# Loading q ahead of k and v for two batches, and scaling the last q of a batch behind the attends

## The chip, the cores and the metric

The kernel runs on one core of one Trainium2 chip. The metric is the device time of one execution in microseconds (us). The mean granted clock of TensorE is 1.000 in the profile of the kernel before. Engines: PE is TensorE, DVE is VectorE, ACT is ScalarE, POOL is GpSimd, SP is SyncE. Spans in a profile are about 1.7 us shorter than the times (986.4 and 988.09 us for the profiled run of the kernel before), because a span runs from the first to the last instruction.

## The reference

```python
# q, k, v: (8 batches, 8 heads, 576, 64)
phi(x) = concat(relu(x) * cos_w, relu(x) * sin_w)      # weights by position
kv  = einsum('bhsf,bhsd->bhfd', phi(k), v);  z = sum_s phi(k)
x   = (phi(q) @ kv) / (phi(q) . z + 1e-6)              # attention, then rows (4608, 512)
P   = sinkhorn(exp(x @ w_gate - max))                  # 8 rounds, 8 experts
out = sum_e P[:, e] * (relu(x @ w1[e]) @ w2[e])
```

The change touches the first stage only, in which the attention of eight batches is computed between the matmuls of the first expert.

## The kernel before

The first stage runs in blocks. Block `j` pushes 512 rows through the first expert's two matmuls in 16 slots: slots 0 to 7 make `h_ps` (four matmuls, then a ReLU on ACT into `hT`; there are two `h_ps` buffers), slots 8 to 15 make `y_ps`. After each slot's matmuls the work listed for that slot is issued, and it belongs to the attention of batch `j + 1` or prepares batch `j + 2`. In these traces an engine takes its work in the written order, so one instruction that waits holds up what stands behind it on its engine; the DVE wait of 2.23 us below, with `zsel` behind it, is an example.

The pieces that matter are these. A load brings two head pairs of q, k or v of one batch (288 KB) and is issued by POOL. `held_back` makes its issue wait for the last DVE instruction written so far. From batch 2 on, a scaled q is transposed by a DMA that SP issues, and there are three scaled-q buffers, so the fourth q waits until the first transpose is done.

Some words for what follows. A DMA has landed when all its data has arrived. The first and second sums of a batch are the key-value sums of its two halves (PE); from their last column DVE makes `zsel`, and "PE's wait for the key sums" is its wait for that `zsel` before the last 12 matmuls of the denominators. `hl` comes from the reciprocal of the denominators. In the profile, transposed q stand under `q_pT`, but two of the eight buffers lie in memory lent by `acc_lo` and `acc_hi` and carry these names, as do other tiles of this stage.

```python
ld      = tile_pool(name="ld", bufs=4)        # 2 batches of each of q, k, v
qp_pool = tile_pool(name="qp_pool", bufs=3)   # scaled q
...
def load(b, half, names="qkv", held_back=False):
    for name in names:
        x = ld.tile([P, 2, C, D], F16, name=f"{name}_ld")
        ...
        i = nc.gpsimd.dma_start(out=..., in_=view[:, 2 * half : 2 * half + 2])
        if held_back:
            after(ve.last, i)                 # wait for the last DVE work written
...
def prep_q(b, hk):
    q16 = loaded.pop(("q", b, hk))
    by_dma = b >= 2
    if by_dma:
        ve.tensor_scalar(out=q16, in0=q16, scalar1=0.0, scalar2=None, op0=ALU.max)
    q_p = qp_pool.tile([P, C, 2, D], F16, name="q_p")
    ve.tensor_tensor(out=q_p[:], in0=q16 (broadcast), in1=cs, op=ALU.mult)
    if by_dma:
        qTs[b, hk] = q_pTs[(b * HK + hk) % len(q_pTs)]
        nc.sync.dma_start(out=qTs[b, hk], in_=q_p[:]..., transpose=True)
...
# prep_k: ReLU of k on ACT.  prep_kv: scaled k and v copy, on DVE.
# sums: key-value sums on PE, `zsel` on DVE.  denominators(b): 24 matmuls over all of
# qTs[b], then a reciprocal on DVE.  attend(b, hk): PE, ACT and DVE write xT.
...
if j == 1:
    for hk in range(HK):
        ...
        at(j, 0, prep_kp, b, hk)
        at(j, (0, 0, 1, 3)[hk], prep_v, b, hk, ...)
        if hk == 1:
            for half in range(2):
                at(j, 0, load, b + 1, half, "qkv", True)
    at(j, 3, sums, b, 0)
    at(j, 5, sums, b, 1)
...
at(j, 6 if j == 1 else 3, denominators, b)
for hk in range(HK):
    at(j, (9, 10, 12, 13)[hk] if j == 1 else 6 + 2 * hk, attend, b, hk)
...
```

The rest of the program, most of its 987 us, is not touched by the change.

The softmax here doesn't subtract the row's maximum and nothing guards it: scores larger than these inputs give would overflow.

## Time and profile before

| | kernel before |
|---|---|
| time, median of 4 runs | 987.46 us (985.78 to 990.17) |
| span of the profile, clock | 986.4 us, 1.000 |
| block 1 (45.68 to 70.25) | 24.57 us |
| block 2 (70.25 to 93.08) | 22.83 us |
| blocks 3 to 5, each | 19.64 us |

A block here reaches from the first `h_ps` matmul of one block to that of the next, read off the timeline of PE. The chain that ended last says how much of the span belongs to whom. This is its line on the page of the kernel before:

```profile
PE 91%; issue 2%; ACT 2%; DVE 2%; DMA 2%; POOL 1%; ACTq 0%; DVEq 0%; POOLq 0%; SPq 0%
```

PE is the chain almost everywhere, so what can be won is PE's idle time. The next lines are the table by stretches of the kernel before, for blocks 1 and 2; the columns are the stretch, its length, the busy time and number of instructions of PE, of weight loads, of DVE, ACT and POOL, then PE's granted clock, the DMA share and GB/s.

```profile
45.68:70.25 24.57, 21.37 (x245) 10.62 (x243) 18.47 (x43) 14.92 (x32) 4.28 (x6) 1.00 0.92 151
70.25:93.08 22.83, 19.88 (x210) 9.99 (x205) 15.59 (x37) 12.59 (x31) 6.59 (x10) 1.00 0.92 133
```

PE stands idle for 3.2 us of block 1 and for 2.95 us of block 2. The timeline of PE in the kernel before shows where. The columns are start, length, engine, line, operation, tiles and shapes, count, and in brackets the idle time before it and what ended it.

```profile
55.16 0.56 PE L109 MATMUL small_ps<-q_pT,zsel 128*32 128x192 f16 x12 [0.72 <-DVE zsel L109]
58.69 0.42 PE L109 MATMUL small_ps<-hl,acc_hi 96*128 96x192 f16 x3 [0.28 <-DVE hl L109]
65.52 0.54 PE L109 MATMUL small_ps<-q_pT,kv_sb 128*64 128x384 f16 x4 [2.06 <-DVE xT L109]
...
79.84 1.02 PE L109 MATMUL h_ps<-xT,w1e 128*128 128x512 f16 x4 [2.19 <-ACT hT L109]
89.23 0.54 PE L109 MATMUL small_ps<-acc_hi,kv_sb 128*64 128x384 f16 x4 [0.76 <-DVE xT L109]
```

PE waited for DVE and ACT, and these in their turn waited for DMAs. These are the lines of the timelines of DVE, ACT and POOL in the kernel before that stand behind the waits:

```profile
53.87 0.31 DVE L109 TENSOR_SCALAR q_ld<-q_ld 128x576 f16<-128x576 f16 x1 [2.23 <-DMA q_ld<-in_q_dram]
64.24 0.76 DVE L109 TENSOR_TENSOR q_p<-q_ld,acc_hi 128x1152 f16<-128x1152 f16 x1 [2.97 <-DMA q_pT<-q_p]
78.62 0.68 ACT L109 ACTIVATE k_ld<-k_ld 128x576 f16<-128x576 f16 x1 [3.32 <-DMA k_ld<-in_k_dram]
49.65 0.72 POOL L201 DMA_DIRECT2D q_ld<-in_q_dram  x1 [16.73 <-DVE k_ld L109]
71.60 0.72 POOL L201 DMA_DIRECT2D q_ld<-in_q_dram  x1 [17.67 <-DVE zsel L109]
```

DVE waits for the first q of batch 3 (53.87), which stands before the `zsel` that PE needs. It waits again for a scaled-q buffer whose transpose has not ended (64.24), with an attend's `xT` behind it. ACT waits for k of batch 4 (78.62), with a ReLU behind it. The loads of batch 3 are issued from 49.65 on and those of batch 4 from 71.60 on. How long the first of them took from issue to landing, and a transpose issued before them, the views of these two tiles tell (POOL's q load at 49.65; SP's transpose at 47.4):

```profile
L201 POOL DMA_DIRECT2D q_ld<-in_q_dram x1: 716/716/716, 49.6 to 49.6; - x1
DMA to landing us min/median/max: 4.2/4.2/4.2
...
L360 SPq DMA_TRANSPOSE q_pT<-q_p x1: 1272/1272/1272, 47.4 to 47.4; - x1
DMA to landing us min/median/max: 4.9/4.9/4.9
```

### The profile page before, as it was taken

The numbers are of one execution on the slowest core, as the hardware profiler recorded it, in microseconds if no ns is written. First come the engines' busy times: TensorE is split into PE (matmuls) and PEld (weight loads), VectorE is DVE, ScalarE is ACT, GpSimd is POOL, SyncE is SP. The second block draws the span as 40 slices with busy tenths as digits, with TensorE's granted clock in tenths as the row PEclk, the third lists the DMA queues.
The fourth block names the chain that finished last, engine by engine and source line by source line (L and its number), as shares of the span: only waits on it lengthen the run. The fifth ranks groups of instructions, "written<-read, shape, count | busy, mean of one in ns | idle before, by whom it ended". The sixth has DMA issues, their size and how long they took to land.

```text
span 986.4 us, 20281 instructions
## 1 busy us (share of the span) xinstructions
PE 968.7 (98%) x7877; PEld 676.4 (69%) x7877; DVE 806.8 (82%) x1833; ACT 565.6 (57%) x1263; POOL 60.6 (6%) x82
## 2 busy tenths in 40 slices
PE   9988999989999999999999999999999999999997
PEld 6544444447777777777777777777777777777775
DVE  6765774789889888988789888988789888988887
ACT  5755665467776555555555555555555555555551
POOL 6122110010000000000000000000000000000001
PEclk9999999999999999999999999999999999999999
DMA  9989990642013410133113400133103401104435
GB/s 164 182 131 161 155 153 21 127 73 61 26 49 68 77 39 25 42 75 68 45 29 67 92 25 26 50 66 68 50 25 67 92 25 27 47 26 116 129 86 129
DMA packets 80336, 73.54 MB, mean 75 GB/s; under 512 B 33264, under 2 KB 72176, under 8 KB 80240
## 3 DMA queue, kind: packets, MB, share of 16 engines
q0 software_dynamic: 27232, 30.94, 20.1%
q1 hardware_dynamic: 52768, 41.06, 17.1%
q8 instruction: 61, 1.00, 0.4%
q14 instruction: 35, 0.29, 0.1%
q10 hardware_dynamic: 240, 0.26, 0.1%
HBM read 83.12 MB, written 12.98 MB: 97 GB/s over the span
## 4 chain that ended last, share of the span: by engine, by line
PE 91%; issue 2%; ACT 2%; DVE 2%; DMA 2%; POOL 1%; ACTq 0%; DVEq 0%; POOLq 0%; SPq 0%
PE rows_ps L109 34%; PE h_ps L109 27%; PE copied_ps L109 11%; PE p_ps L109 11%; PE y_ps L109 5%; PE small_ps L109 3%; DMA q_pT<-q_p 1%; DMA k_ld<-in_k_dram 1%; ACT hT L109 0%; DVE acc_hi L913 0%; POOL hs_last L928 0%; DVE P_tok L109 0%; DMA out_dram<-acc_lo 0%; DVE colp L109 0%; ACT u L109 0%
## 5 line engine op out<-in xcount | busy, mean ns | idle before, releaser
L913 DVE SCALAR_TENSOR_TENSOR acc_lo<-rows_ps,P_tok,acc_lo 128x512 f32<-128x512 f32 (+1 forms) x322 | 203.7, 642 | 74.7 <-PE rows_ps L109 74.6
L109 PEld LDWEIGHTS <-H 128*128 128x128 f16 x2080 | 203.0, 98 | 83.1 <-issue 1.2
L849 ACT CAST u<-h_ps 128x384 f16<-128x384 f32 x288 | 137.8, 479 | 131.1 <-PE h_ps L109 131.1
L109 PEld LDWEIGHTS <-w1e 128*128 128x128 f16 x1632 | 156.5, 98 | 68.9 <-issue 8.7
L843 DVE CUSTOM_DVE_ANT_0 H<-p_ps,u 128x384 f16<-128x384 f32 x329 | 181.6, 552 | 6.5 <-PE p_ps L109 6.4
L109 PEld LDWEIGHTS <-hs 128*128 128x128 f16 x1500 | 146.6, 98 | 56.2
L109 PE MATMUL h_ps<-S,w1e 128*128 128x384 f16 x672 | 164.1, 326 | 1.1 <-ACT u L109 0.9
L109 PE MATMUL p_ps<-xT,T 128*128 128x384 f16 x672 | 164.1, 326 | 0.1
L109 PE MATMUL h_ps<-xT,w1e 128*128 128x384 f16 (+1 forms) x616 | 150.0, 350 | 2.4 <-ACT hT L109 2.2
L109 PE MATMUL rows_ps<-V,H 128*128 128x256 f16 x1000 | 150.0, 273 | 0.7 <-DVE acc_hi L913 0.7
L109 PE MATMUL rows_ps<-w2e,hs 128*128 128x256 f16 x1000 | 150.0, 273 | 0.0
L881 ACT ACTIVATE H<-h_ps 128x384 f16<-128x384 f32 x144 | 70.8, 491 | 95.0 <-PE h_ps L109 95.0
L109 PEld LDWEIGHTS <-T 128*128 128x128 f16 x1008 | 98.1, 98 | 29.3 <-issue 2.8
L109 PE MATMUL rows_ps<-w2e,H 128*128 128x256 f16 (+1 forms) x568 | 91.2, 285 | 0.0
L862 ACT COPY copied_ps<-h_ps 128x384 f32<-128x384 f32 x144 | 67.5, 469 | 35.1 <-PE h_ps L109 35.1
L872 ACT ACTIVATE H<-copied_ps 128x384 f16<-128x384 f32 x144 | 70.9, 493 | 20.3 <-PE copied_ps L109 20.3
L109 PE MATMUL copied_ps<-xT,w1e 128*128 128x384 f16 x336 | 82.1, 326 | 0.0
L109 PE MATMUL h_ps<-S,T 128*128 128x384 f16 x336 | 81.8, 325 | 0.3 <-ACT copied_ps L109 0.3
L109 PE MATMUL copied_ps<-w2e,H 128*128 128x256 f16 x504 | 75.5, 272 | 0.0
L109 PE MATMUL rows_ps<-V,hs 128*128 128x256 f16 x500 | 74.9, 272 | 0.0
L913 DVE SCALAR_TENSOR_TENSOR acc_lo<-copied_ps,P_tok,acc_lo 128x256 f32<-128x256 f32 x126 | 60.3, 478 | 0.4
L913 DVE SCALAR_TENSOR_TENSOR acc_hi<-rows_ps,P_tok,acc_hi 128x512 f32<-128x512 f32 (+1 forms) x56 | 41.3, 738 | 20.5 <-PE rows_ps L109 19.7
(147 smaller groups left out, 955.2 us busy)
## 6 DMA issues: line engine op xcount, KB each, us to landing
S<-x_saved SPq DMA_DIRECT2D x108, 192.0 KB, 2.4
out_dram<-acc_lo SPq DMA_DIRECT2D x62, 128.0 KB, 2.4
w1e<-in_moe_w_dram POOLq DMA_DIRECT2D x7, 1024.0 KB, 9.3
w2e<-in_moe_w_dram POOLq DMA_DIRECT2D x7, 1024.0 KB, 9.6
q_ld<-in_q_dram POOLq DMA_DIRECT2D x16, 288.0 KB, 7.0
k_ld<-in_k_dram POOLq DMA_DIRECT2D x16, 288.0 KB, 8.0
v_ld<-in_v_dram POOLq DMA_DIRECT2D x16, 288.0 KB, 9.1
x_saved<-S SPq DMA_DIRECT2D x18, 192.0 KB, 1.9
```

The lines of the kernel that those rows point to most:

```text
L109: i = getattr(self.engine, name)(*args, **kwargs)
L843: latest = ve._custom_dve(TENSOR_ADD_SAT, out=out, in0=ps[:, 0:TU], in1=t[:], s0=FP32_MAX, s1=0.0)
L849: se.copy(out=t[:], in_=ps[:, 0:TU])
L862: se.copy(out=Y[:, 0:TU], in_=X[:, 0:TU])
L872: se.activation(out=h11, in_=Y[:, 0:TU], func=AF.Relu)
L881: se.activation(out=h12, in_=X[:, 0:TU], func=AF.Relu)
L913: ve.scalar_tensor_tensor(out=a, in0=rows, scalar=P_tok[:, g, self.e : self.e + 1], in1=a, op0=ALU.mult, op1=ALU.add,)
```

## The change

The intent is to have the loads of batches 3 and 4 (the fourth and the fifth) come earlier, with q first, but no earlier than the last scaled q of the batch in front, meant to keep them from overtaking that batch's transposes. The fourth scaled q of batch 3 goes behind all attends of block 1, so that its buffer wait cannot hold up an attend. In block 2 the k scalings are asked for one or two slots later (the first two by two), because k now comes third.

```diff
                 if j == 1:
+                    for name in "qkv":
+                        for half in range(2):
+                            at(j, 0, load, b + 1, half, name, True)
                     for hk in range(HK):
 ...
-                        if hk == 1:
-                            for half in range(2):
-                                at(j, 0, load, b + 1, half, "qkv", True)
 ...
-                    (8, prep_k, 1), (9, prep_q, 3), (10, prep_kv, 0), (10, prep_k, 2),
-                    (12, prep_kv, 1), (12, prep_k, 3), (13, prep_kv, 2), (14, prep_kv, 3),
+                    (8, prep_k, 1), (10, prep_kv, 0), (10, prep_k, 2), (12, prep_kv, 1),
+                    (12, prep_k, 3), (13, prep_q, 3), (14, prep_kv, 2), (14, prep_kv, 3),
                 ) if j == 1 else (
+                    (4, prep_q, 0), (5, prep_k, 0), (5, prep_q, 1), (6, prep_k, 1),
+                    (7, prep_q, 2), (8, prep_kv, 0), (8, prep_k, 2), (9, prep_q, 3),
+                    (10, prep_k, 3), (10, prep_kv, 1), (12, prep_kv, 2), (13, prep_kv, 3),
+                ) if j == 2 else (
                     (3, prep_k, 0), (4, prep_q, 0), (4, prep_k, 1), (5, prep_q, 1),
 ...
-            if j and b + 2 < B:
+            if j == 1:
+                for name in "qkv":
+                    for half in range(2):
+                        at(j, 13, load, b + 2, half, name, True)
+            elif j and b + 2 < B:
                 for half in range(2):
-                    at(j, (14 if j == 1 else 11) + half, load, b + 2, half, "qkv", True)
+                    at(j, 11 + half, load, b + 2, half, "qkv", True)
```

The change has three parts: A, the loads of batch 3; B, the fourth scaled q of batch 3 behind the attends (the third scaled k and v copy moves from slot 13 to 14 with it); C, the loads of batch 4 together with the new order in block 2.

## The prediction

> **What bounds the kernel now.** The chain of waits gives PE 91% of the span, at granted clock 1.000. The change touches only blocks 1 and 2 of the first stage. By the timeline of PE, blocks 3 to 6 last 19.64 us each with PE full; block 1 (45.7 to 70.25) lasts 24.6 us and block 2 (to 93.1) 22.9 us. Block 1 has one half of key-value sums more (0.7 us), so about 7.5 us over PE's own work is all there is to win.
>
> Where it goes (timelines of PE, DVE, ACT):
> - Block 1: DVE waits 2.23 us for q of batch 3 (53.85), delaying the key sums: PE 0.72 us, then 0.28 us for the reciprocal. DVE then waits 2.97 us for a scaled-q buffer whose transpose has not ended (64.2): PE 2.06 us, before an attend.
> - Block 2: ACT waits 3.32 us for k of batch 4 (78.6), holding up the ReLU: PE 2.19 us. A later wait for a transpose costs PE 0.76 us.
>
> **Loads and transposes.** Six loads, issued 0.71 us apart, take about 10.5 us of DMA traffic (51.5 to 62, packets by queue). A transpose alone lands in 3.2 to 3.4 us. One issued at 55.1 under the loads took 9.1: no packet of it moved before 59, then the two queues alternated about one for one. The Trainium skill ("DMA: Bandwidth & Descriptors", queues, rings and completion order) says each engine goes round-robin between its queues by packet; the counts from 59.5 to 61.5 agree, the silence before does not follow from it.
>
> **What the change does.** No operation is added or removed; order and holds differ.
> - Loads of batch 3 start at the last scaled q of batch 2 (DVE ends at 47.3) instead of 49.65. q comes first, both tiles by about 51.5 and 53: no DVE wait, about 1.0 us of PE.
> - The last scaled q of batch 3 goes behind all attends: its buffer is free by then, and a late transpose cannot block an attend: 2.06 us of PE.
> - Loads of batch 4 start at that scaled q, just before block 2 instead of 1.35 us into it. q before k eats part of this, but k is asked for two slots later: ACT's wait falls from 3.3 us to under 1.3, which the two h buffers absorb: about 2 us of PE.
> - Costs. The last transposes of batches 2 and 3 are now released together with the loads: landing goes from 4.9 and 3.2 us to 5 to 7. The denominators need them 6.8 us (block 1) and 5.3 us (block 2) after issue: 0 to 1.5 us, mainly in block 2. q before the last k scalings delays the second sums by 0.2 to 0.4. In block 2 the fourth q's buffer may come later: 0 to 0.5.
>
> Sum: block 1 minus 2.8, block 2 minus 2.0, all on the critical path: -4.8 us. 987.8 becomes **983.0 us**, range **980.0 to 987.0**. Faster by over 2%: 0.01; within 2%: 0.98; slower: 0.01.
>
> **Right if:** block 1 is 21 to 22.3 us and block 2 20 to 21.8; PE's waits of 2.06 and 2.19 us are gone; the first q load is issued near 47.3; blocks 3 to 6 stay 19.64.
>
> **Wrong if:** the denominators wait 2 us or more for a transpose that now shares the engines with the loads; k comes so late behind both q that ACT still holds PE; or spread (985.8 to 990.2) covers the gain.

## The result, and the profile after

The time fell from 987.46 to 983.85 us (medians of 4 runs each; 982.96 to 984.03 after). The ratio is 0.9959, 95% interval 0.9936 to 0.9983. Ratios are the mean time of one kernel's runs over that of the other's of the same rounds, so not quite the ratio of the medians. The interval lies clear of 1. The changed kernel was timed twice more as a control, with ratios 0.9958 and 0.9959.

| | before | after | control 1 | control 2 |
|---|---|---|---|---|
| span of the profile, us | 986.4 | 982.0 | 981.0 | 982.2 |
| start of block 1, us | 45.68 | 45.21 | 44.66 | 45.07 |
| block 1, us | 24.57 | 22.67 | 22.01 | 22.44 |
| block 2, us | 22.83 | 20.78 | 20.76 | 20.92 |

Blocks 1 and 2 together went from 47.40 to 43.45 us, so 3.95 of the 4.4 us by which the spans differ. Most of the rest is the start: block 1 begins 0.47 us earlier in this profile, where the change has done nothing yet. The chain line of the changed kernel and its table by stretches:

```profile
PE 93%; DVE 2%; ACT 2%; DMA 2%; issue 1%; POOL 0%; ACTq 0%; DVEq 0%; SPq 0%; POOLq 0%
...
45.21:67.88 22.67, 20.85 (x245) 10.13 (x244) 17.86 (x41) 14.69 (x32) 4.30 (x6) 1.00 0.97 151
67.88:88.66 20.78, 19.90 (x210) 9.84 (x205) 16.05 (x38) 12.61 (x31) 6.91 (x10) 1.00 1.07 163
```

The chain's share of PE does not tell the two kernels apart: it is 91% and 92% in the controls. PE's busy time in block 1 fell by 0.5 us too, all of it in the small groups of the attends (three of the four `kv_sb` groups show 0.54 us before, all four 0.44 us after); the record does not show how much of this is waiting that the profile counts as work. These are the waits that PE has left in blocks 1 and 2 of the changed kernel, by its timeline:

```profile
55.51 0.56 PE L109 MATMUL small_ps<-q_pT,zsel 128*32 128x192 f16 x12 [1.54 <-DVE zsel L109]
59.04 0.42 PE L109 MATMUL small_ps<-hl,acc_hi 96*128 96x192 f16 x3 [0.28 <-DVE hl L109]
...
69.81 0.46 PE L109 MATMUL small_ps<-acc_lo,k_p 64*128 64x65 f16 x18 [0.50 <-DVE acc_lo L109]
73.95 0.34 PE L109 MATMUL small_ps<-acc_hi,zsel 128*32 128x192 f16 x6 [0.38 <-DMA acc_hi<-q_p]
```

The two long waits (2.06 and 2.19 us) are gone. Two short new ones stand in block 2: the second sums wait for DVE, and the denominators for the last transpose. And one has doubled, from 0.72 to 1.54 us. The reason stands in the timelines of DVE, ACT and POOL:

```profile
54.22 0.31 DVE L109 TENSOR_SCALAR q_ld<-q_ld 128x576 f16<-128x576 f16 x1 [3.05 <-DMA q_ld<-in_q_dram]
77.64 0.68 ACT L109 ACTIVATE k_ld<-k_ld 128x576 f16<-128x576 f16 x1 [0.80 <-DMA k_ld<-in_k_dram]
47.12 1.43 POOL L201 DMA_DIRECT2D q_ld<-in_q_dram  x2 [14.27 <-DVE q_p L109]
68.00 1.43 POOL L201 DMA_DIRECT2D q_ld<-in_q_dram  x2 [16.58 <-DVE q_p L109]
```

The first q load was issued 2.5 us earlier (2.1 us, counted from the start of block 1), and DVE waited longer for it. Its landing time went from 4.2 to 7.1 us, and that of the transpose released with it from 4.9 to 5.9 us:

```profile
L201 POOL DMA_DIRECT2D q_ld<-in_q_dram x1: 713/713/713, 47.1 to 47.1; - x1
DMA to landing us min/median/max: 7.1/7.1/7.1
...
L360 SPq DMA_TRANSPOSE q_pT<-q_p x1: 1272/1272/1272, 46.9 to 46.9; - x1
DMA to landing us min/median/max: 5.9/5.9/5.9
```

So the size of the gain came out about as predicted, but one of its terms did not come: the earlier loads of q were to take a wait away and did not. The experiments ask what each part is worth, and why q came late.

### The profile page after: what moved, and what is told of

It reads as the page before. It is cut to its first block, busy times and chain, and to the rows that moved or that the text cites. A ratio compares the mean times of both kernels' runs of the same rounds, so it can differ in the third digit from the quotient of the medians.

```text
span 982.0 us, 20280 instructions
## 1 busy us (share of the span) xinstructions
PE 967.8 (99%) x7877; PEld 675.3 (69%) x7877; DVE 806.9 (82%) x1833; ACT 564.8 (58%) x1263; POOL 60.7 (6%) x82
## 3 DMA queue, kind: packets, MB, share of 16 engines
q1 hardware_dynamic: 52768, 41.06, 17.1%
## 4 chain that ended last, share of the span: by engine, by line
PE 93%; DVE 2%; ACT 2%; DMA 2%; issue 1%; POOL 0%; ACTq 0%; DVEq 0%; SPq 0%; POOLq 0%
PE rows_ps L109 34%; PE h_ps L109 27%; PE copied_ps L109 11%; PE p_ps L109 11%; PE y_ps L109 6%; PE small_ps L109 4%; DMA q_ld<-in_q_dram 1%; DMA acc_hi<-q_p 1%; ACT hT L109 0%; DVE xT L109 0%; DVE acc_hi L921 0%; POOL hs_last L936 0%; DVE P_tok L109 0%; DMA out_dram<-acc_lo 0%; ACT rb L109 0%
```

## The experiments

Twelve runs were made, two of them of the changed kernel as it is. All gave correct results but one. The runs of one call share their runs of the kernel before. Block lengths come from one profile of each kernel.

### First call: the control and the parts by themselves

The control is the changed kernel, unaltered.

> The changed kernel as it is, a control that shares its runs of the kernel before with the three below. Expected: block 1 (from the first to the second block's first h_ps matmul on PE) 22.7 us, block 2 20.8 us as in its first profile (the kernel before: 24.6 and 22.8), time ratio to before 0.996.

Measured: 982.95 us (982.75 to 983.49, 5 runs) against 987.19 us of the kernel before (986.23 to 988.49, 9 runs), ratio 0.9958 (0.9944 to 0.9971). DVE waited 2.39 us for q, PE 0.87 us for the key sums. The wait for q is thus longer than before in this profile too, but its size varies from run to run.

**Part B alone.** The kernel before, with this edit:

```diff
-                    (8, prep_k, 1), (9, prep_q, 3), (10, prep_kv, 0), (10, prep_k, 2),
-                    (12, prep_kv, 1), (12, prep_k, 3), (13, prep_kv, 2), (14, prep_kv, 3),
+                    (8, prep_k, 1), (10, prep_kv, 0), (10, prep_k, 2), (12, prep_kv, 1),
+                    (12, prep_k, 3), (13, prep_q, 3), (14, prep_kv, 2), (14, prep_kv, 3),
```

> The kernel before with one part of the change: in block 1 the fourth scaled q of batch 3 goes behind all attends (slot 13); loads and block 2 as before. Theory A (the three parts act separately): only PE's 2.06 us wait before an attend goes; the 0.72 us wait for the key sums stays; block 1 22.5 us; block 2 22.8 us with its 2.19 us wait for the ReLU; time 2.0 us below before. Rival B (the 2.06 us wait is only handed on, for instance to the second sums or the denominators of block 2): block 1 plus block 2 fall by under 0.8 us.

Measured: 984.98 us (984.29 to 986.40), ratio 0.9979 (0.9966 to 0.9991), so 2.2 us below before. Block 1 fell to 21.76 us and the 2.06 us wait was gone. Block 2 took 24.01 us, longer than before, although its own wait for the ReLU was about the same (2.06 us). The table by stretches and the timeline of PE of this run show why:

```profile
66.97:90.98 24.01, 21.45 (x210) 10.26 (x205) 16.50 (x38) 12.61 (x31) 7.44 (x11) 0.93 0.96 146
...
77.10 1.30 PE L109 MATMUL h_ps<-xT,w1e 128*128 128x512 f16 x4 [2.06 <-ACT hT L109]
78.19 0.69 PE L109 MATMUL small_ps<-hl,acc_hi 96*128 96x192 f16 x3
78.81 0.69 PE L109 MATMUL small_ps<-q_pT,kv_sb 128*64 128x384 f16 x4
79.44 1.85 PE L109 MATMUL h_ps<-xT,w1e 128*128 128x512 f16 x4
```

After that wait the same groups took 0.69 and 1.85 us that take about 0.41 and 1.04 us elsewhere, and the granted clock of the block was 0.93. The trace's clock records have a stretch at half clock from 77.71 to 81.12. An estimate of its cost is half of 3.41 us, 1.7 us. The edit does not touch this wait; whether a wait of this length draws such a stretch hung on when it fell, as the last section shows. Theory A holds for block 1; the block 2 of this profile can't be compared.

**Part A alone.** The kernel before, with the loads of batch 3 as changed:

```diff
                 if j == 1:
+                    for name in "qkv":
+                        for half in range(2):
+                            at(j, 0, load, b + 1, half, name, True)
 ...
-                        if hk == 1:
-                            for half in range(2):
-                                at(j, 0, load, b + 1, half, "qkv", True)
```

> The kernel before with one part of the change: the loads of batch 3 issued at the last scaled q of batch 2, both q first; the rest as before. Theory A (this part loses by itself, since the first q load now starts together with the last transpose and lands 7 us after issue instead of 4.2): DVE waits about 3.0 us for q, PE 1.5 us for the key sums instead of 0.72, and block 1 is 24.5 to 25.4 us, no better than the 24.6 of before; time 0 to +0.8 us. Rival B (my prediction: the earlier loads win 1.0 us): block 1 23.6 us, time 1.0 us below before.

Measured: 985.53 us (984.79 to 986.12), ratio 0.9982 (0.9970 to 0.9995), so 1.7 us below before, and block 1 24.08 us. Each theory is right in one half. DVE waited 3.07 us for q and PE 1.55 us for the key sums, as theory A said. But the part still gained 0.5 us in block 1, by another way than B had it. The loads of batch 3 ended earlier (the last v landed 17.1 instead of 17.7 us after the start of block 1), so the fourth scaled q got its buffer and started 18.1 instead of 18.6 us after it. PE's wait before the attend was 1.06 instead of 2.06 us: half a microsecond of this is won, the rest has only moved forward to the key sums. Block 2, which this part does not touch, took 22.23 us, 0.6 us less than before; its later wait for a transpose fell from 0.76 to 0.27 us.

**Parts B and C, without A.** The changed kernel, with the loads of batch 3 put back:

```diff
-                    for name in "qkv":
-                        for half in range(2):
-                            at(j, 0, load, b + 1, half, name, True)
 ...
+                        if hk == 1:
+                            for half in range(2):
+                                at(j, 0, load, b + 1, half, "qkv", True)
```

> The changed kernel with the loads of batch 3 put back as they were before (issued after the second v copy of block 1, q k v by halves); all else of the change stays. Theory A: PE's wait for the key sums goes back from 1.54 to about 0.72 us, block 1 about 21.9 us, block 2 as in the changed kernel 20.8 us; time 0.5 to 1.0 us below the changed kernel. Rival B (the early loads of batch 3 are needed, because k and v or the transposes would otherwise come too late for the rest): block 1 22.7 us or more, time the same as or above the changed kernel.

Measured: 983.87 us (983.68 to 985.14), ratio 0.9968 (0.9956 to 0.9981); block 1 22.44 us, block 2 20.77 us. PE's wait for the key sums was 1.31 us, though nothing before it differs from the run of part B alone, where it was 0.62 us. So this wait varies by 0.7 us between profiles of the same work. By time, this kernel lies 0.9 us above the changed one, and theory A had it below. The two intervals overlap, so what part A adds on top of B and C is between nothing and about 1 us, and the profiles do not show by which way.

### Second call: why q lands late

**No transpose beside the load.** The changed kernel: the last transpose of batch 2 is left out and its readers take the one before it. Its output is wrong, which doesn't matter for the time.

```diff
             if by_dma:
+                if (b, hk) == (2, 3):
+                    qTs[b, hk] = qTs[2, 2]
+                    return
                 qTs[b, hk] = q_pTs[(b * HK + hk) % len(q_pTs)]
```

> Wrong on purpose: the changed kernel without the transpose of the last scaled q of batch 2; its readers take the one before it instead, so shapes, counts and holds of all other work stay. It asks why the first q load of batch 3, issued at 47.1, landed 7.1 us later in the changed kernel's profile (another run of it: DVE waited 2.4 us instead of 3.0). Theory A (it shares the DMA engines with that transpose, issued 0.2 us before it): q lands in 4.2 to 5 us, DVE waits under 1.2 us for it, PE's wait for the key sums falls from 0.9 to 1.5 us to nothing, block 1 20.6 to 21.3 us. Rival B (DVE, busy without a pause from 47 to 51, holds back the issuing engine's descriptors) and rival C (six loads at once share the engines): no difference, 6.3 to 7.1 us.

Measured: q landed after 4.4 us, and DVE waited 0.40 us for it. These are the view of the q load's tile and the lines of the table by stretches and of DVE's timeline of this run:

```profile
L201 POOL DMA_DIRECT2D q_ld<-in_q_dram x1: 716/716/716, 47.5 to 47.5; - x1
DMA to landing us min/median/max: 4.4/4.4/4.4
...
45.60:66.12 20.52, 20.52 (x245) 10.26 (x243) 18.02 (x41) 14.52 (x32) 4.28 (x6) 1.00 1.00 152
...
51.95 0.31 DVE L109 TENSOR_SCALAR q_ld<-q_ld 128x576 f16<-128x576 f16 x1 [0.40 <-DMA q_ld<-in_q_dram]
```

PE had no wait at all in block 1: 20.52 of 20.52 us busy. DVE was as busy as in the changed kernel (4.0 of the 4.1 us from the first q load's issue on, in both) and all six loads were there, so rivals B and C fall: it is the transpose. Rival B was worth a try, since the Trainium skill ("DMA: Bandwidth & Descriptors", SWDGE vs HWDGE vs iDMA) says that POOL writes its descriptors into the same memory from which DVE can lock it out; no run here shows that as a delay. By time, 982.93 us (982.59 to 983.31, 4 runs), ratio 0.9957 (0.9940 to 0.9974), the kernel shows none of the 1.5 to 2.1 us that its block 1 is shorter; but that interval, about 1.7 us to either side, is too wide to rule such a gain out. In the profiles the gain is there: from the start of block 1 to the end of the span this kernel took 935.3 us, the changed one 936.4 to 937.1 (three profiles). What hides it is the start of block 1, at 45.60 here and at 44.66 to 45.21 there, before any edit acts.

**The old hold, q first.** The changed kernel, with the loads of batch 3 held as before but in the new order:

```diff
-                    for name in "qkv":
-                        for half in range(2):
-                            at(j, 0, load, b + 1, half, name, True)
 ...
+                        if hk == 1:
+                            for name in "qkv":
+                                for half in range(2):
+                                    at(j, 0, load, b + 1, half, name, True)
```

> The changed kernel with only the hold of batch 3's loads as before (after the second v copy of block 1, near 49.0) but both q first. Theory A (sharing with the transpose costs what the earlier issue wins): the first q lands 4.2 us after its issue, near 53.3, no later than in the changed kernel (53.0 to 54.2) though it is issued 2 us later; DVE waits 2 to 2.7 us; block 1 22.0 to 22.4 us; time within 1 us of the changed kernel. Rival C (the six loads themselves delay q): 6 to 7 us after issue, near 55.5, DVE waits over 4 us, block 1 over 23.5 us.

Measured: q was issued at 49.0 and landed 4.2 us later, at 53.2; DVE waited 2.23 us, block 1 took 22.20 us, block 2 20.84 us. Time 984.10 us (983.56 to 984.43, 4 runs), ratio 0.9967 (0.9953 to 0.9982). This is theory A to the number. Over all the profiles of correct kernels: where the first q of batch 3 was issued 0.2 us behind the last transpose of batch 2 it took 6.3 to 7.6 us (six profiles, among them those of both controls and of two kernels below), and where it was issued 2.3 us behind it 4.1 to 4.8 us (four profiles). Counted from the start of block 1, q landed after 8.2 to 9.5 us in the first group and 8.1 to 8.8 us in the second. The earlier issue won nothing for q. The first q load of batch 4 shows the same: 5.7 to 6.2 us where it was issued 0.1 to 0.2 us behind the last transpose of batch 3 (eight profiles), 4.2 to 4.3 us where it came 2 us or more behind it (four profiles).

**The new loads of batch 4, the old order of block 2.** The changed kernel without the list of its own for block 2:

```diff
                 ) if j == 1 else (
-                    (4, prep_q, 0), (5, prep_k, 0), (5, prep_q, 1), (6, prep_k, 1),
-                    (7, prep_q, 2), (8, prep_kv, 0), (8, prep_k, 2), (9, prep_q, 3),
-                    (10, prep_k, 3), (10, prep_kv, 1), (12, prep_kv, 2), (13, prep_kv, 3),
-                ) if j == 2 else (
                     (3, prep_k, 0), (4, prep_q, 0), (4, prep_k, 1), (5, prep_q, 1),
```

> The changed kernel with the preparations of block 2 in the order of before (k scaling asked for at slot 3, not 5); loads as changed. Theory A (the win of block 2 is the two slots of grace, because k comes third in line now and lands about as late, 9.7 us into block 2, as it did before, 8.3): ACT waits over 3.5 us for k, PE 2 to 3 us for the ReLU, block 2 23 us or more, and time 2.3 us above the changed kernel, more where the clock drops. Rival B (the earlier issue of the loads is what wins block 2): ACT waits under 2 us and block 2 stays under 21.5 us.

Measured: 987.22 us (985.82 to 990.73, 6 runs), ratio 1.0002 (0.9986 to 1.0019): the whole gain of the change is gone. ACT waited for k longer than in the kernel before, and PE with it, as the timelines of ACT and PE of this run show:

```profile
79.98 0.68 ACT L109 ACTIVATE k_ld<-k_ld 128x576 f16<-128x576 f16 x1 [4.55 <-DMA k_ld<-in_k_dram]
...
76.22 0.35 PE L109 MATMUL small_ps<-acc_hi,zsel 128*32 128x192 f16 x6 [0.82 <-DMA acc_hi<-q_p]
81.20 1.75 PE L109 MATMUL h_ps<-xT,w1e 128*128 128x512 f16 x4 [2.42 <-ACT hT L109]
```

Block 2 took 25.36 us and block 1 24.39 us; each has a stretch of 3.41 us at half clock in it. Rival B falls: earlier loads alone do not win block 2. A part of the loss is lost clock, and block 1, whose work this edit leaves alone, has one of the two stretches: the profiled run is the slowest of the six; by the record the two runs with a mean clock of 0.999 took 985.82 and 986.16 us, the four with 0.996 to 0.998 took 987.16 to 990.73 us. k, now third in line, landed 10.2 us into block 2 here (8.3 in the kernel before).

**A version that might beat both.** The two q loads of batch 3 alone are issued earlier still, at the second scaled q of batch 2, so that q is there when block 1 asks for it:

```diff
-                    for name in "qkv":
+                    for name in "kv":
                         for half in range(2):
                             at(j, 0, load, b + 1, half, name, True)
 ...
                     at(j, slot, fn, b + 1, hk, *args)
+                for half in range(2):
+                    at(j, 12, load, b + 2, half, "q", True)
```

> A version that might beat both: the changed kernel with the two q loads of batch 3 alone issued earlier still, at the second scaled q of batch 2 (near 43), four us before k and v. Theory A (q is late in block 1 because its loads start together with the last transpose and behind nothing else): q is there by 50, DVE does not wait for it, PE's wait for the key sums goes (0.9 to 1.5 us), as does the wait of ACT for k (2.5 us, absorbed); block 1 20.6 to 21.3 us, time 1.0 to 1.5 us below the changed kernel. Rival D (the loads now hold up the transposes of batch 2, which the denominators of block 1 need): PE waits for a transpose before the 12-matmul group of the denominators, block 1 over 22 us.

Measured: 996.77 us (994.77 to 998.44, 6 runs), ratio 1.0095 (1.0080 to 1.0111). Theory A is wrong about this kernel and rival D right, by more than it said. q landed at 49.2, in time. But the transposes of batch 2 now came behind it and then among the loads of k and v. The view of the last transpose's tile and the timeline of PE of this run:

```profile
L360 SPq DMA_TRANSPOSE q_pT<-q_p x1: 4366/4366/4366, 46.6 to 46.6; - x1
DMA to landing us min/median/max: 18.0/18.0/18.0
...
55.81 0.42 PE L109 MATMUL small_ps<-q_pT,zsel 128*32 128x192 f16 x6 [2.41 <-DMA q_pT<-q_p]
64.66 0.51 PE L109 MATMUL small_ps<-q_pT,zsel 128*32 128x192 f16 x6 [8.43 <-DMA q_pT<-q_p]
```

The transpose took 18.0 us, PE stood 10.8 us before the denominators, the clock fell to a half for 13.65 us, and block 1 took 34.11 us. This is what the hold at the last scaled q protects against.

### Third call: the other half of block 2, and a finer hold

The control again:

> The changed kernel once more, unaltered, as the control on the same chip for the three below. Expected: block 1 22.0 to 22.7 us with a wait of PE for the key sums of 0.9 to 1.6 us, block 2 20.8 us; time ratio to before 0.996.

Measured: 983.21 us (982.65 to 983.91, 5 runs) against 987.45 us (985.63 to 989.46, 9 runs), ratio 0.9959 (0.9946 to 0.9972); q wait 2.82 us, PE's wait for the key sums 1.31 us.

**The new order of block 2, the old loads of batch 4.** The changed kernel with this edit:

```diff
-            if j == 1:
-                for name in "qkv":
-                    for half in range(2):
-                        at(j, 13, load, b + 2, half, name, True)
-            elif j and b + 2 < B:
+            if j and b + 2 < B:
                 for half in range(2):
-                    at(j, 11 + half, load, b + 2, half, "qkv", True)
+                    at(j, (14 if j == 1 else 11) + half, load, b + 2, half, "qkv", True)
```

> The changed kernel with the loads of batch 4 as before (halves q k v, at slots 14 and 15 of block 1); the preparations of block 2 stay in the changed order. With the run that had the changed loads and the order of before (PE waited 2.4 us for the ReLU and 0.8 for a transpose) it completes a two by two. Theory A (the two slots of grace alone win block 2, the earlier loads add nothing): k lands about 8.3 us into block 2, is asked for near 7, ACT waits under 1.8 us, PE does not wait for the ReLU, and the 0.38 us wait for the transpose of the last q goes; block 2 20.4 to 21.2 us, time within 0.7 us of the changed kernel. Rival B (both parts are needed): PE waits 0.8 us or more for the ReLU or for a later transpose, block 2 over 21.5 us, time 1 us or more above the changed kernel.

Measured: 985.03 us (983.84 to 986.24, 5 runs), ratio 0.9978 (0.9963 to 0.9993), 1.8 us above the control; two of the five runs (986.05 and 986.24) ran at a mean clock of 0.997 and 0.998. PE did not wait for the ReLU (ACT 0.54 us for k), nor for the transpose before the denominators. But the loads ended later, so the transposes of batch 4 came later, and the fourth q waited for its buffer again, as the timelines of PE and DVE show:

```profile
85.46 0.54 PE L109 MATMUL small_ps<-acc_hi,kv_sb 128*64 128x384 f16 x4 [1.07 <-DVE xT L109]
...
84.18 0.76 DVE L109 TENSOR_TENSOR q_p<-q_ld,acc_hi 128x1152 f16<-128x1152 f16 x1 [1.48 <-DMA q_pT<-q_p]
```

Block 2 took 21.47 us. Rival B is nearer: the order takes the ReLU's wait away by itself, the earlier loads take the later wait for a transpose, and only both together give 20.8 us.

**Both holds a little later.** Loads and transposes should start apart, by one scaled k and one v copy:

```diff
-                    for name in "qkv":
-                        for half in range(2):
-                            at(j, 0, load, b + 1, half, name, True)
 ...
+                        if hk == 0:
+                            for name in "qkv":
+                                for half in range(2):
+                                    at(j, 0, load, b + 1, half, name, True)
 ...
-                    (12, prep_k, 3), (13, prep_q, 3), (14, prep_kv, 2), (14, prep_kv, 3),
+                    (12, prep_k, 3), (13, prep_q, 3), (13, prep_kv, 2), (14, prep_kv, 3),
```

> A version that might beat both: the changed kernel with both holds one scaled k and one v copy later (about 0.7 to 1.0 us), so that the transpose released at the old hold has its packets through before the first load's. Theory A (loads and transpose delay each other where they start together): the first q of batch 3 is issued near 47.8 and lands in 4.2 to 5.2 us, by 53; PE waits under 0.7 us for the key sums; the last transpose of batch 3 lands in under 5 us and PE does not wait for it; block 1 21.0 to 21.9 us, block 2 20.2 to 20.8 us, time 0.5 to 1.5 us below the changed kernel. Rival C (what delays q is the number of loads in flight): q lands as late as in the changed kernel or later, block 1 22.0 us and up, time not below it.

Measured: the mechanism did as theory A said, the time did not. q was issued at 48.7 and landed 4.9 us later, PE waited 0.43 us for the key sums, the last transpose of batch 3 landed in 3.2 us and PE did not wait for it. Block 1 fell to 21.76 us. But k of batch 4 came later, ACT waited 1.91 us for it, PE 0.51 us for ACT, and block 2 rose to 21.25 us. Time 983.46 us (982.92 to 984.12), ratio 0.9962 (0.9949 to 0.9975): the same as the control.

**The same, with the scaled k and v copies of batch 3 one step earlier** (against the changed kernel; the new hold of the loads of batch 3, as above, is left out here):

```diff
 ...
-                    (8, prep_k, 1), (10, prep_kv, 0), (10, prep_k, 2), (12, prep_kv, 1),
-                    (12, prep_k, 3), (13, prep_q, 3), (14, prep_kv, 2), (14, prep_kv, 3),
+                    (8, prep_k, 1), (9, prep_kv, 0), (10, prep_kv, 1), (10, prep_k, 2),
+                    (12, prep_kv, 2), (12, prep_k, 3), (13, prep_q, 3), (14, prep_kv, 3),
 ...
-                        at(j, 13, load, b + 2, half, name, True)
+                        at(j, 14, load, b + 2, half, name, True)
```

> The one above with the scaled k and v copies of batch 3 one step earlier in block 1 (slots 9, 10, 12, 14 instead of 10, 12, 13, 14), to fill DVE's idle time of 0.76 and 0.60 us before the second and third attend; the loads of batch 4 then hang on the last v copy. Expected if DVE's backlog at the end of block 1 is what makes PE wait 0.50 us for the second sums: that wait goes, block 2 20.0 to 20.4 us, time 0.3 to 0.6 us below the one above. Rival: v or k is not there yet at slot 9 or 10, DVE waits for it before an attend, and block 1 grows by 0.5 us or more.

Measured: 983.92 us (983.06 to 985.31), ratio 0.9967 (0.9951 to 0.9983), no better. The 0.50 us wait for the second sums went, as expected, and DVE waited for no k or v before an attend. But in this profile q took 6.5 us to land although it was issued 1.2 us behind the transpose; PE waited 1.97 us for the key sums, the clock fell to a half for 3.41 us right after, and block 1 took 24.20 us. The profile of block 2 (20.95 us) has an ACT wait for k of 2.29 us.

No version tried beats the changed kernel.

## Why the prediction was right or wrong

The total was right: 983.0 us was predicted, in a range of 980.0 to 987.0, and 983.85 us measured (982.95 and 983.21 in the controls). The gain was put at 4.8 us; by the medians it was 3.6 us, and 4.2 us in both controls. The range reaches from nearly no gain to 7.5 us, so the total alone tests little; the terms do.

- **The wait of 2.06 us before an attend goes.** Right. Part B alone removed it and brought block 1 to 21.76 us and the time down by 2.2 us.
- **Block 2 wins about 2 us, because k is asked for two slots later and ACT's wait falls under 1.3 us.** Right in size: 2.05 us, with ACT waiting 0.80, 0.88 and 1.07 us in the three profiles. The two by two of block 2 shows that the order and the loads are both needed. With the loads alone ACT waited 4.55 us and by the medians the whole gain was lost, in part to half clock; with the order alone 21.47 us remained.
- **"q comes first, both tiles by about 51.5 and 53: no DVE wait, about 1.0 us of PE."** Wrong, and this is the step that failed. The first tile landed at 54.2 and DVE waited 3.05 us (2.39 and 2.82 in the controls; 2.23 before). PE's wait for the key sums was 0.9 to 1.5 us instead of nothing. The term was minus 1.0 us and measured plus 0.15 to 0.8 us against the one profile of the kernel before. With the old hold this wait was 0.62 to 1.31 us over four profiles, so that the term won nothing is shown, that it lost is not. I had counted the cost of starting loads and a transpose together only for the transpose (5 to 7 us to land, and 5.9 and 6.0 us it was), and had the load land about 4.2 us after its issue, as it had when issued 2.3 us behind the transpose. Without that transpose it took 4.4 us; issued 0.2 us behind it 6.3 to 7.6 us.
- **Costs in block 2.** About right: PE waited 0.38 us for the transpose of the last q (put at 0 to 1.5 us) and 0.50 us for the second sums (put at 0.2 to 0.4 us). DVE waited 0.21 us for the fourth q's buffer.
- **Block 1 would be 21 to 22.3 us.** 22.67, 22.01 and 22.44 us: at the upper edge and over it, by the failed term. That it fell so far was in part luck: of the 1.90 us in the first profile the terms give 1.24 (2.06 won, 0.82 lost). The other 0.66 us, 0.52 of it PE's shorter busy time and 0.15 a gap too short to be listed as a wait, stands in no term of the prediction.
- **The first q load is issued near 47.3.** 47.12. **Blocks 3 to 6 stay 19.64 us.** Blocks 3 to 5 did, but for block 4, which was 20.04 and 20.18 us in the controls. Block 6 was misread: it lasts 18.76 us, before and after.

Open are three things. By time, part A is worth 1.7 us alone and about 0.9 us on top of the others, and for the latter no profile shows the way. In the last kernel q took 6.5 us although it was issued 1.2 us behind the transpose, where the run above it had 4.9 us. And the times of the kernel before spread from 985.0 to 990.2 us (33 runs) against 982.7 to 984.0 us (14 runs) of the changed one.

Stretches at half clock behind waits of about 2 us are only a small part of that spread. The record gives the mean clock of 29 runs of the kernel before: 18 ran at 0.997 or 0.998 and took 987.5 us in the mean, the other 11, at 0.999 or 1.000, took 986.9 us. One stretch of 3.41 us at half clock lowers the mean clock by about 0.0017, and all runs of the changed kernel show 0.999 or 1.000. By an estimate from these means, such stretches make about 0.4 us of the 4 us between the kernels. The seven runs of the kernel before at 1.000 alone reach from 985.0 to 988.8 us, and what spreads these is open.

## What to carry to other kernels

When a load is moved to start earlier, look at what else starts then: its landing time in the old trace holds for the neighbours it had there, and a collision costs both sides. Have what is needed first loaded first, but move the point where the displaced tile is asked for as well, or the wait only changes its name. On an engine that works in order, a wait costs little at the end of a group of work and much in front of what another engine needs: here, putting one scaled q behind the attends was worth 2.2 us by itself, about as much as the rest of the change added to it (2.0 us).

## What the Trainium skill lacked or had wrong

- "DMA: Bandwidth & Descriptors" says (queues, rings and completion order) that each DMA engine goes round-robin between its queues by packet. It has no figure for what a load pays beside a transpose: here 6.3 to 7.6 us to land instead of 4.1 to 4.8 us, if issued 0.2 us behind it.
- Round-robin alone does not give what a transpose pays that is issued under six loads: in the kernel before it took 9.1 us instead of 3.2, and from 55.1 to 59 no packet of it moved. With loads on both sides of it, 18.0 us. No page has this.
- The same page (why a DMA increments its semaphore by 16) says that each of the 16 engines counts for itself. The trace agrees, and shows what a transpose does to the counts: of the first q load of the changed kernel 12 of the 16 had come by 52.11 us, the others at 52.65, 53.02, 53.38 and 54.19; without the transpose all 16 came from 51.33 to 51.93. The trace does not name the engines, and no run shows why a few are late.
- "TensorE: Matmul & The Clock Gate" (The HAM clock gate; Why this matters for your kernels) gives a free-running window of about 3.4 us and advises against PE idle gaps over about 3 us. Here shorter ones were enough. By the trace's clock records the stretches at half clock have the length of 3.41 us or a multiple of it, and start on a grid of that step. Five of them came after a wait of 1.94 to 2.42 us that fell into one step of the grid (in four different kernels). No such stretch came after the waits of 2.06 and 2.19 us of the kernel before, which a step's edge cut into pieces of at most 1.61 us; and in none of the 14 profiles did a stretch start after a step with 1.6 us of idle time or less.
